# An attention-plus-rational kernel: rational part in four VectorE steps between copies, loads issued first, edge zeroing moved to VectorE, last batch copied by ScalarE

## The chip, the cores and the metric

The kernel runs on one core of one Trainium2 chip. The metric is the device time of one execution in microseconds (us); lower is better. Most executions of a kernel agree within 1%. A traced execution's span is about 1.8 us shorter than the time that is measured for it, because the time also counts what lies outside the span.

## The reference, cut to what matters

Eight batches, twelve heads, 448 positions, head dimension 64. Softmax attention with an extra term in the denominator, then a two-layer block with a rational function in the middle.

```python
scores = scale * q @ k^T                  # per batch and head, 448 x 448
e = exp(scores - m)
attn = e / (sum(e) + exp(-m) + 1e-9)
x = (attn @ v)                            # heads side by side: 3584 x 768
h = x @ w_in                              # 3584 x 2048
P = a[0] + a[1]*h + a[2]*h**2 + a[3]*h**3
Q = 1 + |b[0]|*|h| + |b[1]|*h**2
out = (P / (Q + 1e-6)) @ w_out            # 3584 x 768
```

## The kernel before

A list of work items with times is sorted, and this fixes the program order; TensorE (PE) and ScalarE (ACT) keep that order, while the framework's scheduler orders VectorE (DVE), GpSimd (POOL) and SyncE (SP). So the source alone does not tell where an instruction lands in VectorE's or GpSimd's queue; the compiled program does. Six pairs of heads per batch are one unit of attention; the first GEMM of batch b runs beside the attention of batch b+1, the second GEMM a batch later.

Batches 0 and 1 are transposed on TensorE. From batch 2 on, GpSimd loads k and q (`k4`, `q4`) and SyncE transposes them by DMA into `kT` and `qT`. `q4` has a zero column block at each end. It is zeroed again each time that a batch gets a new `q4` from the pool of two, so the zeroing has to wait until the buffer's former contents have been read:

```python
def load(b, h0=0, h1=H):
    if h0 == 0:
        q4 = ld.tile([T, D + H * NJ * D + D], F16, tag="q4", name="q4")   # pool ld: bufs=2
        nc.gpsimd.memset(q4[:, 0:D], 0.0)
        nc.gpsimd.memset(q4[:, D + H * NJ * D:], 0.0)
        ...                                  # k4, v4, qT, kT: 2 buffers each
    nc.gpsimd.dma_start(out=k4..., in_=runs(k))
    nc.gpsimd.dma_start(out=q4[:, D + h0 * w:D + h1 * w]..., in_=runs(q))
    nc.gpsimd.dma_start(out=v4..., in_=runs(v))

def transpose_dma(b):                        # on SyncE, in order
    nc.sync.dma_start_transpose(out=kT..., in_=k4)
    nc.sync.dma_start_transpose(out=qT[:, T:]..., in_=q4[:, D:D + H * NJ * D])
    nc.sync.dma_start_transpose(out=qT[:, 0:2 * nb * T]..., in_=q4[:, 0:H * NJ * D])
    nc.sync.dma_start_transpose(out=qT[:, 2 * nb * T:]..., in_=q4[:, H * NJ * D:])
```

VectorE copies the first GEMM's result from PSUM, the memory that holds the kernel's matmul results (`h<-hp`), multiplies the attention output by the reciprocal denominator (`xt<-u,rden`), computes the rational part's polynomials on groups of four column blocks (eight instructions, plus `g<-w,c`), and copies the second GEMM's result (`osb<-op`). `hp`, `op` and the transposes share a pool of two PSUM buffers; `u` has one.

```python
    h = hts[b][:, fc % FG, :]
    if b < B - 1 or fc % 2:
        nc.vector.tensor_copy(out=h, in_=hp[:, 0:S])
    else:
        nc.scalar.activation(out=h, in_=hp[:, 0:S], func=AF.Copy)
    ...                                      # every fourth fc: denominator(), eight VectorE instructions
# the schedule
work.append((n - 0.7, transpose_pair, (b, p)))         # b < 2
work.append((n + 1.02, attend, (b, p)))
work.append((t0 + fc * NP / NFC, gemm1, (b, fc)))
work.append((1.0, load_w_out, ()))
```

The softmax here doesn't subtract the row's maximum and nothing guards it: scores larger than these inputs give would overflow.

Of the kernel before, what the change touches and what calls it, by code (L numbers as in the profile page):

```python
# [9 lines left out]
F16 = mybir.dt.float16  # L10
U16 = mybir.dt.uint16
AF = mybir.ActivationFunctionType
ALU = mybir.AluOpType
# [3 lines left out]
def kernel(  # L17
# [11 lines left out]
    nc = tc.nc  # L29

    B, H, S, D = q.shape
    DM, FF = moe_w_in.shape
    NP = H // 2
    NJ = 4
    T = S // NJ
    assert T <= 128 and T % 16 == 0 and D == 64
    NFC = FF // 128
    NDC = DM // 128
    HD = DM // 2
    FG = 4  # L40
# [12 lines left out]
    moe = ctx.enter_context(tc.tile_pool(name="moe", bufs=2))  # L53
# [9 lines left out]
    def load(b, h0=0, h1=H):  # L63
        if h0 == 0:
            q4 = ld.tile([T, D + H * NJ * D + D], F16, tag="q4", name="q4")
            nc.gpsimd.memset(q4[:, 0:D], 0.0)
            nc.gpsimd.memset(q4[:, D + H * NJ * D:], 0.0)
            loaded[b] = (
                q4,
                ld.tile([T, H * NJ * D], F16, tag="k4", name="k4"),  # L70
                ld.tile([T, H, NJ, D], F16, tag="v4", name="v4", bufs=2),
                ld.tile([128, (1 + H * NJ) * T], F16, tag="qT", name="qT", bufs=2),
                ld.tile([128, H * NJ // 2 * T], F16, tag="kT", name="kT", bufs=2),
            )
        q4, k4, v4, _, _ = loaded[b]
        w = NJ * D

        def runs(src):
            return src[b, h0:h1].rearrange("h (p j) d -> p h (j d)", j=NJ)

        nc.gpsimd.dma_start(
            out=k4[:, h0 * w:h1 * w].rearrange("p (h x) -> p h x", x=w), in_=runs(k))
        nc.gpsimd.dma_start(
            out=q4[:, D + h0 * w:D + h1 * w].rearrange("p (h x) -> p h x", x=w),
            in_=runs(q))
        nc.gpsimd.dma_start(
            out=v4[:, h0:h1].rearrange("p h j d -> p h (j d)"), in_=runs(v))
# [21 lines left out]
    def transpose_pair(b, p):  # L109
# [12 lines left out]
                                k4[:, 2 * g * D:(2 * g + 2) * D], ident[0:T, 0:T])  # L122
        nc.vector.tensor_copy(out=kT[:, 4 * p * T:4 * (p + 1) * T], in_=tk)  # L123


    ones = const.tile([T, 64], F16)
    nc.vector.memset(ones, 1.0)
    ident = const.tile([128, 128], F16)
    make_identity(nc, ident)
    abc = const.tile([128, 4], F32)  # L130
    nc.sync.dma_start(out=abc, in_=moe_a.unsqueeze(0).to_broadcast([128, 4]))
    bbc = const.tile([128, 2], F32)
# [3 lines left out]
        out=babs, in0=bbc, scalar1=-1.0, scalar2=None, op0=ALU.mult  # L136
# [6 lines left out]
    a0, a1, a2, a3 = (abc[:, i:i + 1] for i in range(4))  # L143
# [5 lines left out]
    def load_w_in(i, n):  # L149
        f = slice(FF * i // n, FF * (i + 1) // n)  # L150
        nc.gpsimd.dma_start(
            out=w_in_sb[:, :, f],
            in_=moe_w_in[:, f].rearrange("(c p) f -> p c f", p=128))
# [51 lines left out]
    hts = {}  # L205

    def gemm1(b, fc):
        xt = xts[b]
        hp = ps.tile([128, 512], F32, tag="gen", bufs=2, name="hp")
        for c in range(NDC):  # L210
            nc.tensor.matmul(  # L211
                out=hp[:, 0:S], lhsT=w_in_sb[:, c, fc * 128:(fc + 1) * 128],
                rhs=xt[:, c, :], start=(c == 0), stop=(c == NDC - 1),
            )
        if fc % FG == 0:
            hts[b] = moe.tile([128, FG, S], F16, tag="h", name="h")
            gs[b, fc // FG] = gp.tile([128, FG, S], F16, tag="g", name="g")
        h = hts[b][:, fc % FG, :]
        if b < B - 1 or fc % 2:
            nc.vector.tensor_copy(out=h, in_=hp[:, 0:S])  # L220
        else:
            nc.scalar.activation(out=h, in_=hp[:, 0:S], func=AF.Copy)
        for f0, n in groups(b, fc // FG):
            if fc % FG == f0 + n - 1:
                denominator(b, fc // FG, f0, n)


    def groups(b, gi):
        last = b == B - 1 and gi == NG - 1
        return [(0, FG // 2), (FG // 2, FG // 2)] if last else [(0, FG)]  # L230

    cs = {}
    ns = {}


    def denominator(b, gi, f0, n):
        f = slice(f0, f0 + n)
        h = hts[b][:, f, :]
        w = moe.tile([128, FG, S], F16, tag="w", name="w")[:, f, :]
        c = moe.tile([128, FG, S], F16, tag="c", name="c")[:, f, :]  # L240
        nc.vector.tensor_scalar(out=w.bitcast(U16), in0=h.bitcast(U16),
                                scalar1=0x7FFF, scalar2=None, op0=ALU.bitwise_and)
        nc.vector.tensor_scalar(out=c, in0=w, scalar1=b1, scalar2=b0,  # L243
                                op0=ALU.mult, op1=ALU.add)
        nc.vector.tensor_tensor(out=c, in0=c, in1=w, op=ALU.mult)  # L245
        n = w
        nc.vector.tensor_scalar(out=n, in0=h, scalar1=a3, scalar2=a2,  # L247
                                op0=ALU.mult, op1=ALU.add)
        nc.vector.tensor_tensor(out=n, in0=n, in1=h, op=ALU.mult)  # L249
        nc.vector.tensor_scalar(out=n, in0=n, scalar1=a1, scalar2=None, op0=ALU.add)  # L250
        nc.vector.tensor_tensor(out=n, in0=n, in1=h, op=ALU.mult)  # L251
        nc.vector.tensor_scalar(out=n, in0=n, scalar1=a0, scalar2=None, op0=ALU.add)
        cs[b, gi, f0] = c
        ns[b, gi, f0] = n


    def log(b, gi, f0, n):
# [23 lines left out]
    def store(b, c0, n, src):  # L281
        dst = out[b * S:(b + 1) * S, :].rearrange("(p j) d -> j p d", j=NJ)
        r = 0
        while r < n:
            j, p0 = divmod(c0 + r, T)
            m = min(T - p0, n - r)
            nc.sync.dma_start(out=dst[j, p0:p0 + m], in_=src[r:r + m, :])
            r += m

    def gemm2(b, tl, nh):  # L290
        if tl < NW:
            def lhs(fc):
                return gs[b, fc // FG][:, fc % FG, tl * 128:(tl + 1) * 128]
        else:
            def lhs(fc):
                return gxs[b][:, fc, :]
        if nh == 0:
            osbs[b, tl] = moe.tile([128, DM], F32, tag="osb", name="osb")
        osb = osbs[b, tl]
        op = ps.tile([128, 512], F32, tag="gen", bufs=2, name="op")  # L300
        for fc in range(NFC):
            nc.tensor.matmul(  # L302
                out=op[:, 0:HD], lhsT=lhs(fc),
                rhs=w_out_sb[:, fc, nh * HD:(nh + 1) * HD],
                start=(fc == 0), stop=(fc == NFC - 1),
            )
        nc.vector.tensor_copy(out=osb[:, nh * HD:(nh + 1) * HD], in_=op[:, 0:HD])  # L307
        if nh == 1:
            if tl < NW:
                store(b, tl * 128, 128, osb)  # L310
            else:
                store(b - 1, SM, SR, osb[0:SR])
                store(b, SM, SR, osb[SR:128])
# [1 line left out]



    for h0 in range(0, H, 3):
        load(0, h0, h0 + 3)
    load_w_in(0, 2)  # L320
    load(1, 0, 6)
    load_w_in(1, 2)
    load(1, 6, H)


    slots = [n + o for n in range(B * NP) for o in (0.1, 0.6)]
    slots += [B * NP + 0.5 + 0.25 * i for i in range(60)]

    work = []
    for b in range(B):  # L330
        if b >= 2:
            work.append((b * NP - NP - 1.5, load, (b,)))
            work.append((b * NP - NP - 1.49, transpose_dma, (b,)))
        for p in range(NP):
            n = b * NP + p
            if b < 2:
                work.append((n - 0.7, transpose_pair, (b, p)))
            for at, h, i in ((0.0, 2 * p, 0), (0.0, 2 * p, 1),
                             (0.5, 2 * p + 1, 0), (0.5, 2 * p + 1, 1)):
                work.append((n + at, scores, (b, h, i)))  # L340
            work.append((n + 1.02, attend, (b, p)))
        t0 = (b + 1) * NP + 1.4
        for fc in range(NFC):
            work.append((t0 + fc * NP / NFC, gemm1, (b, fc)))
            for f0, n in groups(b, fc // FG):
                if fc % FG == f0 + n - 1:
                    ready = t0 + fc * NP / NFC + 0.3
                    for step in (log, quotient):
                        while slots[0] < ready:
                            slots.pop(0)  # L350
                        work.append((slots.pop(0), step, (b, fc // FG, f0, n)))
        t0 = (b + 2) * NP + 3.0
        work.append((t0 - 0.1, left_over, (b,)))
        tiles = list(range(NW)) + ([NW] if b % 2 else [])
        units = [(b, tl, nh) for tl in tiles for nh in range(2)]
        for i, args in enumerate(units):
            work.append((t0 + i * NP / len(units), gemm2, args))
# [34 lines left out]
```

## Time and profile before

| | before |
|---|---|
| time, median of 4 runs | 504.42 us (502.55 to 506.12) |
| span of the traced run | 501.8 us |
| TensorE busy | 455.0 us, 91% |
| VectorE busy | 374.5 us, 75% |
| ScalarE busy | 326.7 us, 65% |

TensorE bounds the kernel. The page's second part shows the span in 40 equal slices (a digit is the busy share in tenths, 9 is 90% or more). It is full from the eighth slice (about 88 us) on, but for the end. It loses time before that, above all in the first 60 us, where the DMA engines are busy for nine tenths of the time or more, and again near the end, where VectorE is the full one:

```profile
PE   3877978999999999999999999999999999999785
DVE  1223579998969688796969688886969689899921
DMA  9999999998598109931681109811011101111122
```

The waits table (who waited <- for whom: us in total, times, longest us) has these lines for GpSimd. Its zeroing of `q4` (L66) waits for DMA transposes of an earlier batch: `q_420` is batch 2, `q_885` batch 3, `q_1384` batch 4, `q_1979` batch 5, `q_2576` batch 6, `q_3171` batch 7.

```profile
POOL q_1979 L66 <- DMA qT<-q_885: 23.4, 1, 23.4
POOL q_885 L66 <- DMA qT<-q_420: 16.3, 1, 16.3
POOL q_2576 L66 <- DMA qT<-q_1384: 14.3, 1, 14.3
POOL q_3171 L66 <- DMA qT<-q_1979: 13.1, 1, 13.1
```

GpSimd has little else to do (10% busy), so these 67 us cost little there. When the transposes land is shown by the chain of waits in order of time (start us, duration us, what), for batch 2, followed by the first scores that use them. Batch 2's k takes 26.56 us to land; its transposes land at 85.96 us; TensorE's first scores of batch 2 start at 86.09 us, after a wait of 1.2 us:

```profile
33.90 26.56 DMA k_423<-in_k_dram
60.48 4.29 SPq L96
64.82 3.73 SPq L98
68.59 17.37 DMA qT<-q_420
86.09 0.41 PE sps L170 x2
```

For the last batch, the stretches view (from:to and length, then busy us of each engine with the number of instructions, the granted TensorE clock, DMA share and GB/s) shows VectorE full and then TensorE at 0.79 of its clock:

```profile
455.00:470.00 15.00, 11.53 (x66) 6.17 (x64) 14.93 (x24) 7.29 (x8) 1.58 (x2) 1.00 0.09 27
470.00:478.00 8.00, 6.19 (x28) 3.09 (x26) 6.77 (x14) 1.99 (x2) 0.00 (x0) 0.79 0.17 49
```

### The profile page before, as it was taken

The numbers are of one execution on the slowest core, as the hardware profiler recorded it, in microseconds if no ns is written. First come the engines' busy times: TensorE is split into PE (matmuls) and PEld (weight loads), VectorE is DVE, ScalarE is ACT, GpSimd is POOL, SyncE is SP. The second block draws the span as 40 slices with busy tenths as digits, with TensorE's granted clock in tenths as the row PEclk, the third lists the DMA queues.
The fourth block names the chain that finished last, engine by engine and source line by source line (L and its number), as shares of the span: only waits on it lengthen the run. The fifth ranks groups of instructions, "written<-read, shape, count | busy, mean of one in ns | idle before, by whom it ended". The sixth has DMA issues, their size and how long they took to land.

```text
span 501.8 us, 7259 instructions
## 1 busy us (share of the span) xinstructions
PE 455.0 (91%) x2962; PEld 225.6 (45%) x2962; DVE 374.5 (75%) x550; ACT 326.7 (65%) x363; POOL 52.3 (10%) x93
## 2 busy tenths in 40 slices
PE   3877978999999999999999999999999999999785
PEld 2343434445444444444444444444444444555353
DVE  1223579998969688796969688886969689899921
ACT  2797668887776876667776876667776864336300
POOL 9410010401101001010010000010000000100000
PEclk9999989999999999999999999999999999999899
DMA  9999999998598109931681109811011101111122
GB/s 123 206 205 208 204 156 177 161 169 145 110 147 141 31 3 175 186 67 31 98 157 33 33 0 166 122 31 33 2 32 33 31 1 31 45 51 33 30 65 63
DMA packets 91089, 46.85 MB, mean 93 GB/s; under 512 B 51632, under 2 KB 85936, under 8 KB 91056
## 3 DMA queue, kind: packets, MB, share of 16 engines
q0 software_dynamic: 36464, 22.81, 33.3%
q1 hardware_dynamic: 54592, 23.58, 23.9%
q8 instruction: 23, 0.38, 0.3%
q14 instruction: 10, 0.08, 0.0%
HBM read 45.62 MB, written 11.01 MB: 113 GB/s over the span
## 4 chain that ended last, share of the span: by engine, by line
PE 42%; DVE 27%; ACT 13%; DMA 10%; issue 5%; SPq 2%; POOL 1%; DVEq 0%; POOLq 0%
PE op L302 21%; PE hp L211 10%; ACT e L175 6%; DMA k_423<-in_k_dram 5%; DVE h L220 5%; PE sps L170 4%; PE den L188 4%; DMA qT<-q_420 3%; DVE c L245 3%; PE u L188 3%; DVE w L249 3%; DVE xt L199 2%; DVE osb L307 2%; ACT c L263 2%; DVE c L243 2%
## 5 line engine op out<-in xcount | busy, mean ns | idle before, releaser
L175 ACT ACTIVATE e<-sps 112x896 f16<-112x896 f32 x192 | 164.4, 912 | 105.2 <-PE sps L170 105.0
L211 PE MATMUL hp<-xt,w_in_sb 128*128 128x448 f16 x768 | 163.4, 354 | 5.6 <-DVE qT L117 2.7
L302 PE MATMUL op<-w_out_sb,g 128*128 128x384 f16 x768 | 133.4, 329 | 14.5 <-DVE h L220 9.5
L211 PEld LDWEIGHTS <-w_in_sb 128*128 128x128 f16 x768 | 68.4, 97 | 90.6 <-issue 37.3
L302 PEld LDWEIGHTS <-g 128*128 128x128 f16 x768 | 75.5, 98 | 71.4 <-issue 20.0
L220 DVE CAST h<-hp 128x448 f16<-128x448 f32 x120 | 72.9, 618 | 8.9 <-PE hp L211 8.3
L170 PE MATMUL sps<-qT,kT 64*112 64x448 f16 x384 | 61.9, 384 | 12.0 <-DVE kT L123 4.7
L199 DVE TENSOR_TENSOR xt<-u,rden 128x448 f16<-128x448 f32 x48 | 29.8, 621 | 55.7 <-ACT rden L196 23.3
L259 ACT ACTIVATE c<-c,oneeps_c 128x1792 f16<-128x1792 f16 (+1 forms) x33 | 57.3, 1737 | 20.5 <-DVE c L245 20.5
L264 DVE TENSOR_TENSOR g<-w,c 128x1792 f16<-128x1792 f16 (+1 forms) x33 | 35.4, 1074 | 25.5 <-issue 15.4
L263 ACT ACTIVATE c<-c 128x1792 f16<-128x1792 f16 (+1 forms) x33 | 54.2, 1644 | 0.2
L188 PE MATMUL den<-e,ones 112*64 112x448 f16 x384 | 47.0, 368 | 0.0
L307 DVE COPY osb<-op 128x384 f32<-128x384 f32 x56 | 30.9, 552 | 18.0 <-PE op L302 16.6
L170 PEld LDWEIGHTS <-kT 64*112 64x112 f16 x384 | 20.0, 127 | 48.2 <-issue 37.7
L278 POOL COPY gx<-g 128x256 f16<-128x256 f16 x32 | 15.5, 504 | 229.5 <-DVE g L264 203.1
L245 DVE TENSOR_TENSOR c<-c,w 128x1792 f16<-128x1792 f16 (+1 forms) x33 | 35.2, 1067 | 1.0
L251 DVE TENSOR_TENSOR w<-w,h 128x1792 f16<-128x1792 f16 (+1 forms) x33 | 35.1, 1063 | 0.8
L249 DVE TENSOR_TENSOR w<-w,h 128x1792 f16<-128x1792 f16 (+1 forms) x33 | 34.9, 1057 | 0.5
L195 ACT ACTIVATE rden<-den,one_c 128x448 f32<-128x448 f32 x48 | 30.8, 642 | 5.2 <-PE den L188 5.2
L196 ACT ACTIVATE rden<-rden 128x448 f32<-128x448 f32 x48 | 27.7, 577 | 1.5
L188 PEld LDWEIGHTS <-ones 112*64 112x64 f16 x384 | 18.0, 111 | 22.1 <-issue 15.1
L247 DVE TENSOR_SCALAR w<-h,abc 128x1792 f16<-128x1792 f16 (+1 forms) x33 | 24.2, 732 | 0.7
(87 smaller groups left out, 269.2 us busy)
## 6 DMA issues: line engine op xcount, KB each, us to landing
w_in_sb<-in_moe_w_in_dram POOLq DMA_DIRECT2D x2, 1536.0 KB, 18.0
w_out_sb<-in_moe_w_out_dram POOLq DMA_DIRECT2D x1, 3072.0 KB, 32.9
out_dram<-osb SPq DMA_DIRECT2D x8, 336.0 KB, 2.7
out_dram<-osb SPq DMA_DIRECT2D x8, 288.0 KB, 4.1
out_dram<-osb SPq DMA_DIRECT2D x8, 240.0 KB, 2.6
out_dram<-osb SPq DMA_DIRECT2D x8, 192.0 KB, 2.7
out_dram<-osb SPq DMA_DIRECT2D x8, 144.0 KB, 2.5
out_dram<-osb SPq DMA_DIRECT2D x8, 96.0 KB, 3.9
```

The lines of the kernel that those rows point to most:

```text
L170: nc.tensor.matmul(out=sps[0:T, half, 0:S], lhsT=kT[r, (2 * h + i) * T:(2 * h + i + 1) * T], rhs=qT[r, c:c + S], start=True, stop=True,)
L175: nc.scalar.activation(out=e, in_=sps[0:T, :, 0:S], func=AF.Exp, scale=scale)
L188: nc.tensor.matmul(out=dst[64 * hh:64 * hh + 64, 0:S], lhsT=w(hh, j), rhs=e[hh, j // 2][:, j % 2, :], start=(j == 0), stop=(j == NJ - 1), ...
L199: nc.vector.tensor_tensor(out=xts[b][:, p, :], in0=u[:, 0:S], in1=rden, op=ALU.mult)
L211: nc.tensor.matmul(out=hp[:, 0:S], lhsT=w_in_sb[:, c, fc * 128:(fc + 1) * 128], rhs=xt[:, c, :], start=(c == 0), stop=(c == NDC - 1),)
L220: nc.vector.tensor_copy(out=h, in_=hp[:, 0:S])
L245: nc.vector.tensor_tensor(out=c, in0=c, in1=w, op=ALU.mult)
L249: nc.vector.tensor_tensor(out=n, in0=n, in1=h, op=ALU.mult)
L259: nc.scalar.activation(out=c, in_=c, func=AF.Ln, bias=oneeps_c)
L263: nc.scalar.activation(out=c, in_=c, func=AF.Exp, scale=-1.0)
L302: nc.tensor.matmul(out=op[:, 0:HD], lhsT=lhs(fc), rhs=w_out_sb[:, fc, nh * HD:(nh + 1) * HD], start=(fc == 0), stop=(fc == NFC - 1),)
L307: nc.vector.tensor_copy(out=osb[:, nh * HD:(nh + 1) * HD], in_=op[:, 0:HD])
```

## The change

Its intent: PSUM copies should not wait behind eight rational instructions in a row, so the rational part becomes four items placed between copies; loads start before the constants are made; transposes move a little earlier; in the last batch, where VectorE is full, ScalarE takes all copies, and the first GEMM is drawn together so that more of the second GEMM is left to cover the last rational part. The zeroing of `q4` goes to VectorE so that GpSimd is free to issue loads.

```diff
-            nc.gpsimd.memset(q4[:, 0:D], 0.0)
-            nc.gpsimd.memset(q4[:, D + H * NJ * D:], 0.0)
+            nc.vector.memset(q4[:, 0:D], 0.0)
+            nc.vector.memset(q4[:, D + H * NJ * D:], 0.0)
 ...
+    load(0, 0, 3)                       # ahead of the constants; the other three thirds behind ident
 ...
-        if b < B - 1 or fc % 2:
+        if b < B - 1:
             nc.vector.tensor_copy(out=h, in_=hp[:, 0:S])
         else:
             nc.scalar.activation(out=h, in_=hp[:, 0:S], func=AF.Copy)
-        for f0, n in groups(b, fc // FG):
-            if fc % FG == f0 + n - 1:
-                denominator(b, fc // FG, f0, n)
 ...                                     # denominator() cut into den_0, den_1, num_0, num_1
-        nc.vector.tensor_copy(out=osb[:, nh * HD:(nh + 1) * HD], in_=op[:, 0:HD])
+        o = osb[:, nh * HD:(nh + 1) * HD]
+        if b < B - 1:
+            nc.vector.tensor_copy(out=o, in_=op[:, 0:HD])
+        else:
+            nc.scalar.activation(out=o, in_=op[:, 0:HD], func=AF.Copy)
 ...
-                work.append((n - 0.7, transpose_pair, (b, p)))
+                work.append((n - 0.95, transpose_pair, (b, p)))
 ...
+        step1 = NP / NFC if b < B - 1 else 0.3
         for fc in range(NFC):
-            work.append((t0 + fc * NP / NFC, gemm1, (b, fc)))
+            work.append((t0 + fc * step1, gemm1, (b, fc)))
 ...
+                    for dt, part in ((0.02, den_0), (0.1, den_1), (0.4, num_0),
+                                     (0.75, num_1)):
+                        work.append((t + dt * (n / FG), part, args))
```

Before the run, the compiled program could already be read. This is VectorE's queue in the changed kernel, by position; `DMAHW` are semaphores of SyncE's DMAs, `DMASW` of GpSimd's. Position 34 is batch 3's zeroing. It waits for batch 2's q load and its three q transposes, because batch 3's `q4` was given batch 2's buffer, and it stands ahead of batch 1's first `xt`:

```
32 L117 TensorCopy qT<-tq 128x896 [waits PE]
33 L123 TensorCopy kT<-tk 128x448 [waits PE]
34 L66 Memset q_882 112x32 [waits DMAHW4,DMAHW3,DMAHW5,DMASW6,DVE]
35 L67 Memset q_882 112x32
36 L203 TensorTensor xt<-u,rden 128x448 [waits PE,Activation]
37 L117 TensorCopy qT<-tq 128x896 [waits PE]
```

More of the change, by code (lines that the diff above doesn't have):

```diff
@@ L129 @@
     make_identity(nc, ident)
+    for h0 in range(3, H, 3):
+        load(0, h0, h0 + 3)
     abc = const.tile([128, 4], F32)
@@ L215, in gemm1 @@
         if fc % FG == 0:
-            hts[b] = moe.tile([128, FG, S], F16, tag="h", name="h")
+            hts[b, fc // FG] = moe.tile([128, FG, S], F16, tag="h", name="h")
             gs[b, fc // FG] = gp.tile([128, FG, S], F16, tag="g", name="g")
-        h = hts[b][:, fc % FG, :]
-        if b < B - 1 or fc % 2:
+        h = hts[b, fc // FG][:, fc % FG, :]
+        if b < B - 1:
             nc.vector.tensor_copy(out=h, in_=hp[:, 0:S])
@@ L233, with chunk, temp, den_0 @@
     ns = {}
-    def denominator(b, gi, f0, n):
-        f = slice(f0, f0 + n)
-        h = hts[b][:, f, :]
-        w = moe.tile([128, FG, S], F16, tag="w", name="w")[:, f, :]
-        c = moe.tile([128, FG, S], F16, tag="c", name="c")[:, f, :]
+    def chunk(b, gi, f0, n):
+        return hts[b, gi][:, f0:f0 + n, :]
+    def temp(tag, f0, n):
+        return moe.tile([128, FG, S], F16, tag=tag, name=tag)[:, f0:f0 + n, :]
+    def den_0(b, gi, f0, n):
+        h, w, c = chunk(b, gi, f0, n), temp("w", f0, n), temp("c", f0, n)
         nc.vector.tensor_scalar(out=w.bitcast(U16), in0=h.bitcast(U16),
@@ L244, in denominator, with den_1, num_0, num_1 @@
                                 op0=ALU.mult, op1=ALU.add)
-        nc.vector.tensor_tensor(out=c, in0=c, in1=w, op=ALU.mult)
-        n = w
-        nc.vector.tensor_scalar(out=n, in0=h, scalar1=a3, scalar2=a2,
-                                op0=ALU.mult, op1=ALU.add)
-        nc.vector.tensor_tensor(out=n, in0=n, in1=h, op=ALU.mult)
-        nc.vector.tensor_scalar(out=n, in0=n, scalar1=a1, scalar2=None, op0=ALU.add)
-        nc.vector.tensor_tensor(out=n, in0=n, in1=h, op=ALU.mult)
-        nc.vector.tensor_scalar(out=n, in0=n, scalar1=a0, scalar2=None, op0=ALU.add)
-        cs[b, gi, f0] = c
-        ns[b, gi, f0] = n
+        ns[b, gi, f0] = w
+        cs[b, gi, f0] = c
+    def den_1(b, gi, f0, n):
+        c = cs[b, gi, f0]
+        nc.vector.tensor_tensor(out=c, in0=c, in1=ns[b, gi, f0], op=ALU.mult)
+    def num_0(b, gi, f0, n):
+        h, m = chunk(b, gi, f0, n), ns[b, gi, f0]
+        nc.vector.tensor_scalar(out=m, in0=h, scalar1=a3, scalar2=a2,
+                                op0=ALU.mult, op1=ALU.add)
+        nc.vector.tensor_tensor(out=m, in0=m, in1=h, op=ALU.mult)
+    def num_1(b, gi, f0, n):
+        h, m = chunk(b, gi, f0, n), ns[b, gi, f0]
+        nc.vector.tensor_scalar(out=m, in0=m, scalar1=a1, scalar2=None, op0=ALU.add)
+        nc.vector.tensor_tensor(out=m, in0=m, in1=h, op=ALU.mult)
+        nc.vector.tensor_scalar(out=m, in0=m, scalar1=a0, scalar2=None, op0=ALU.add)
     def log(b, gi, f0, n):
@@ L313, in gemm2 @@
                 store(b, SM, SR, osb[SR:128])
-    for h0 in range(0, H, 3):
-        load(0, h0, h0 + 3)
     load_w_in(0, 2)
@@ L342 @@
         t0 = (b + 1) * NP + 1.4
+        step1 = NP / NFC if b < B - 1 else 0.3
         for fc in range(NFC):
-            work.append((t0 + fc * NP / NFC, gemm1, (b, fc)))
+            work.append((t0 + fc * step1, gemm1, (b, fc)))
             for f0, n in groups(b, fc // FG):
                 if fc % FG == f0 + n - 1:
-                    ready = t0 + fc * NP / NFC + 0.3
+                    args = (b, fc // FG, f0, n)
+                    t = t0 + fc * step1
+                    for dt, part in ((0.02, den_0), (0.1, den_1), (0.4, num_0),
+                                     (0.75, num_1)):
+                        work.append((t + dt * (n / FG), part, args))
+                    ready = t + 0.5 * n / FG
                     for step in (log, quotient):
@@ L350 @@
                             slots.pop(0)
-                        work.append((slots.pop(0), step, (b, fc // FG, f0, n)))
+                        work.append((slots.pop(0), step, args))
         t0 = (b + 2) * NP + 3.0
```

## The prediction

> **What bounds the kernel now.** TensorE: 455.0 us busy of a 501.8 us span (page, part 1), about 58 of every 60 us between 100 and 400 us (stretches). VectorE is 75% busy. TensorE loses time in the first 60 us, and at the end, where VectorE bounds (14.93 of 15 us busy at 455 to 470 us; TensorE waits 2.99 and 1.82 us, then runs 28 matmuls in 6.39 us instead of about 4.5).
>
> **What the change is meant to give.** Steady state: little. By the compiled order TensorE's sequence is nearly the same up to the last batch, and VectorE's queue already had the rational steps between copies; the waits open to gain (op on h 9.9 us in the waits table, osb 5.6 us) may shrink by 2 us. End: ScalarE takes 8 more h copies (0.62 us each on VectorE) and the last 8 osb copies (0.55 us), and more second-GEMM work covers the last rational chain: 3 to 8 us less. Start: first load 0.7 us sooner.
>
> **What it costs.** The zeroing of q4's edges moves from GpSimd to VectorE. Under 0.2 us per batch itself, but it must wait until the buffer's old contents have been read. In the before trace GpSimd waits there harmlessly: 16.3, 23.4, 14.3 and 13.1 us, each ended by the DMA transposes of an earlier batch's q (waits table). The compiled order keeps these waits and puts them early into VectorE's queue: batch 3's memset right behind the PSUM copies of batch 1's second pair, ahead of batch 1's first xt multiply; batches 5, 6, 7 two to six instructions behind the last xt of batches 1, 2, 3. The Trainium skill, "TensorE: Matmul & The Clock Gate" (Architectural detail), says VectorE is strictly FIFO; so everything behind stops.
>
> - Batch 3: VectorE arrives at about 45 us; the transposes of batch 2 land at 86.3 us in the before trace, held by DMA loads (batch 2's k lands at 60.5 us), which the change doesn't speed up. TensorE stops at its first first-GEMM unit (49.3 us before, for want of a PSUM buffer) and resumes near 87: 38 us lost.
> - Batch 5: the transposes start when batch 1's last scores free kT (82.5 us in before's time) and take about 24 us; VectorE arrives some 10 us after that start. TensorE loses about 11 us.
> - Batches 6, 7: transposes 129.9 to 153.2 and 186.9 to 208.8 us; VectorE arrives near 141 and 198 us. Stalls of 12 and 11 us; TensorE loses 9 to 10 each.
> - After each stop TensorE runs about 4 us at half speed (same page, "The HAM clock gate": cold after an idle window of about 3.4 us; this trace agrees: den x8 takes 1.71 us early on, 0.95 later): 1.5 to 2 us each.
>
> TensorE has no slack to recover, so all is on the critical path. 38 + 11 + 10 + 9 + 7 = 75 us, less about 9 us at end and start, and 1 to 3 us of DMA waits that vanish: 503 + 63 = 566 us.
>
> **What the profile would show.** Waits table: VectorE memset of q4 waiting on DMA qT, once about 40 us and three times 8 to 14. TensorE idle from about 50 to 86 us; short gaps in the next 130 us; VectorE's busy sum hardly changed; no VectorE-bound stretch at the end.
>
> **What would make it wrong.** Transposes that land much sooner, now that q loads are no longer held; VectorE working off its backlog within TensorE's slack, halving the three later losses; ScalarE's last copies stuck behind its logarithms, eating the gain at the end.
>
> Predicted 566 us, 546 to 584 eight times in ten. Faster by over 2%: 0.04; within 2%: 0.03; slower: 0.93.

## The result, and the profile after

The changed kernel takes 565.62 us (median of 4 runs, 565.39 to 566.46) against 504.42 us, a ratio of 1.1217 (95% interval 1.1167 to 1.1268): 12% slower.

| | before | after |
|---|---|---|
| time | 504.42 us | 565.62 us |
| span of the traced run | 501.8 us | 564.0 us |
| TensorE busy | 455.0 us, 91% | 460.2 us, 82% |
| VectorE busy | 374.5 us, 75% | 366.4 us, 65% |
| mean granted TensorE clock | 0.992 | 0.934 |

VectorE has 8 us less to do and ScalarE 7 us more (333.7 us), the copies of the last batch; TensorE's 5 us more are the same 2962 matmuls, some at a lower clock. None of that is 61 us. The slices show a hole of three slices near the start, and three shallower dents behind it (in both PE and DVE):

```profile
PE   4873009883799769995999999999999999998896
DVE  1231004991989459782788888787878887989920
```

The waits table now has the zeroing's waits on VectorE (`q_882` is batch 3, `q_1976` batch 5, `q_2573` batch 6, `q_3168` batch 7), and TensorE waiting behind it:

```profile
DVE q_882 L66 <- DMA qT<-q_420: 39.4, 1, 39.4
DVE q_1976 L66 <- DMA qT<-q_882: 12.6, 1, 12.6
DVE q_2573 L66 <- DMA qT<-q_1381: 12.4, 1, 12.4
DVE q_3168 L66 <- DMA qT<-q_1976: 10.5, 1, 10.5
PE hp L215 <- DVE qT L117: 39.1, 4, 37.4
PE hp L215 <- DVE h L224: 26.5, 3, 12.1
```

The first stop in the timeline (start us, duration us, engine, line, operation, and in brackets the idle time before it and what ended it). VectorE does its last copy at 44.27 us; the memset, which takes 0.09 us itself, runs at 84.08 us; TensorE resumes at 85.38 us, and its six matmuls take 2.40 us, where they took 1.29 us in the kernel before:

```profile
44.27 0.38 DVE L123 COPY kT<-tk 128x448 f16<-128x448 f16 x1
47.66 0.36 PE L121 MATMUL tk<-ident,k_120 112*128 112x112 f16 x4
84.08 0.09 DVE L66 MEMSET q_882<- 112x32 uint32 x1 [39.43 <-DMA qT<-q_420]
84.17 0.62 DVE L203 TENSOR_TENSOR xt<-u,rden 128x448 f16<-128x448 f32 x1
85.38 2.40 PE L215 MATMUL hp<-xt,w_in_sb 128*128 128x448 f16 x6 [37.36 <-DVE qT L117]
```

How much each stop cost can be read from one recurring event: SyncE starts the transposes of batch b+2 when batch b's last scores have freed `kT`. The starts, from SyncE's timeline:

| kT transpose of batch | before | after | later by | added since the line above |
|---|---|---|---|---|
| 3 (batch 1's scores done) | 82.51 | 117.75 | 35.24 | 35.2: first stop |
| 4 (batch 2's) | 129.86 | 178.07 | 48.21 | 13.0: second |
| 5 (batch 3's) | 186.89 | 245.24 | 58.35 | 10.1: third |
| 6 (batch 4's) | 243.04 | 309.53 | 66.49 | 8.1: fourth |
| 7 (batch 5's) | 300.01 | 366.51 | 66.50 | 0.0 |

The four stops cost 66.5 us; the spans differ by 62.2 us, so 4.3 us were won back, all in the last batch (the last `u` group is still 66.5 us late, at 485.48 against 418.98 us). In the steady stretch the change gains nothing at all. This is one such stretch of the kernel before and its counterpart after, 42.23 us each, with the same busy time to the hundredth on every engine:

```profile
257.78:300.01 42.23, 41.06 (x269) 19.89 (x266) 33.69 (x49) 30.42 (x35) 0.81 (x2) 1.00 0.15 36
```

```profile
324.28:366.51 42.23, 41.06 (x269) 19.89 (x266) 33.69 (x49) 30.42 (x35) 0.81 (x2) 1.00 0.17 37
```

### The profile page after: what moved, and what is told of

Same layout as the page of the kernel before. It is cut to its first block, busy times and chain, and to the rows that moved or that the text cites. A ratio compares the mean times of both kernels' runs of the same rounds, so it can differ in the third digit from the quotient of the medians.

```text
span 564.0 us, 7256 instructions
## 1 busy us (share of the span) xinstructions
PE 460.2 (82%) x2962; PEld 227.0 (40%) x2962; DVE 366.4 (65%) x550; ACT 333.7 (59%) x379; POOL 50.5 (9%) x77
## 4 chain that ended last, share of the span: by engine, by line
PE 38%; DVE 23%; DMA 12%; SPq 10%; ACT 9%; issue 5%; POOL 2%; DVEq 0%; POOLq 0%
PE op L314 17%; PE hp L215 13%; SPq L101 6%; DMA k_423<-in_k_dram 5%; ACT e L179 4%; DVE h L224 4%; PE sps L174 3%; PE den L192 3%; DVE c L253 3%; DMA k_120<-in_k_dram 3%; SPq L98 2%; DVE w L260 2%; PE u L192 2%; ACT c L275 2%; DVE g L276 2%
## 5 line engine op out<-in xcount | busy, mean ns | idle before, releaser
L215 PE MATMUL hp<-xt,w_in_sb 128*128 128x448 f16 x768 | 170.0, 365 | 68.2 <-DVE qT L117 39.1
L314 PE MATMUL op<-w_out_sb,g 128*128 128x384 f16 x768 | 131.5, 326 | 12.2 <-DVE h L224 9.9
L215 PEld LDWEIGHTS <-w_in_sb 128*128 128x128 f16 x768 | 70.5, 100 | 157.0 <-issue 106.4
L224 DVE CAST h<-hp 128x448 f16<-128x448 f32 x112 | 68.3, 618 | 10.6 <-PE hp L215 10.0
L174 PE MATMUL sps<-qT,kT 64*112 64x448 f16 x384 | 62.2, 386 | 11.0 <-ACT e L179 4.8
L192 PEld LDWEIGHTS <-ones 112*64 112x64 f16 x384 | 17.9, 110 | 22.3 <-issue 15.3
L321 DVE COPY osb<-op 128x384 f32<-128x384 f32 x48 | 26.4, 550 | 0.7 <-PE op L314 0.7
L66 DVE MEMSET q_882<- 112x32 uint32 x1 | 0.1, 85 | 39.4 <-DMA qT<-q_420 39.4
```

The source lines that it names most:

```text
L174: nc.tensor.matmul(out=sps[0:T, half, 0:S], lhsT=kT[r, (2 * h + i) * T:(2 * h + i + 1) * T], rhs=qT[r, c:c + S], start=True, stop=True,)
L192: nc.tensor.matmul(out=dst[64 * hh:64 * hh + 64, 0:S], lhsT=w(hh, j), rhs=e[hh, j // 2][:, j % 2, :], start=(j == 0), stop=(j == NJ - 1), ...
L215: nc.tensor.matmul(out=hp[:, 0:S], lhsT=w_in_sb[:, c, fc * 128:(fc + 1) * 128], rhs=xt[:, c, :], start=(c == 0), stop=(c == NDC - 1),)
L314: nc.tensor.matmul(out=op[:, 0:HD], lhsT=lhs(fc), rhs=w_out_sb[:, fc, nh * HD:(nh + 1) * HD], start=(fc == 0), stop=(fc == NFC - 1),)
```

## The experiments

Theory: the time is lost because the zeroing's wait for DMA transposes now stands in VectorE's queue, which is strictly in order; what it costs is set by when those transposes land. Rivals: the new order of rational steps and copies, or ScalarE's copies, cost the time; or there is a fixed cost of zeroing on VectorE. Ten kernels were run; all gave correct results.

### e1: the zeroing back on GpSimd, all else as changed

```diff
-            nc.vector.memset(q4[:, 0:D], 0.0)
-            nc.vector.memset(q4[:, D + H * NJ * D:], 0.0)
+            nc.gpsimd.memset(q4[:, 0:D], 0.0)
+            nc.gpsimd.memset(q4[:, D + H * NJ * D:], 0.0)
```

> The changed kernel with one thing undone: the zeroing of q4's edges is back on GpSimd. Theory (the waits of the memset stop VectorE's queue): the 66.5 us lost between 45 and 310 us vanish, the 4 us won at the end stay: 496 to 500 us; no VectorE wait on a DMA transpose; GpSimd waits 10 to 25 us on them again. Rival (the new order of the rational steps, or ScalarE's copies, cost the time, and VectorE's waits only show up where TensorE would have waited anyway): above 550 us.

Measured: 501.65 us (500.66 to 502.18, 6 runs), ratio 0.996 (0.9942 to 0.9978). The loss is gone with this one edit, and the rival falls. But the time misses the upper end of the expectation by 1.7 us. The waits table tells where a part of it went: TensorE now waits 4.9 us for batch 2's transposes, where the kernel before waited 1.2 us. Above it stands GpSimd's line; it waits again, as expected:

```profile
POOL q L66 <- DMA qT<-q: 67.2, 4, 24.1
PE sps L174 <- DMA qT<-q: 4.9, 1, 4.9
```

### e2: the kernel before with the zeroing on VectorE

The reverse edit, on the kernel before.

> The kernel before with one thing done: the zeroing moved to VectorE, nothing else. Theory: 503 plus about 66 us, 566 to 573 us, with VectorE waits on DMA transposes of about 40, 12, 12 and 10 us. Rival: within 1% of 503 us.

Measured: 571.31 us (570.05 to 572.9, 4 runs), ratio 1.1335 (1.1304 to 1.1366). As the theory has it; the four waits are 38.4, 11.5, 12.4 and 11.3 us. The two lines that move the zeroing make the whole loss, without any other part of the change.

### e3: two q4 buffers kept for the whole run and zeroed once, on VectorE

```diff
+    q4s = []
+    for i in range(2):
+        q4s.append(const.tile([T, D + H * NJ * D + D], F16, name=f"q4{i}"))
+        nc.vector.memset(q4s[i][:, 0:D], 0.0)
+        nc.vector.memset(q4s[i][:, D + H * NJ * D:], 0.0)
 ...
-            q4 = ld.tile([T, D + H * NJ * D + D], F16, tag="q4", name="q4")
-            nc.vector.memset(q4[:, 0:D], 0.0)
-            nc.vector.memset(q4[:, D + H * NJ * D:], 0.0)
+            q4 = q4s[b % 2]
```

> The changed kernel with two q4 buffers that are kept for the whole run and zeroed once at the start, on VectorE, so that the zeroing never has to wait for a reader. Theory (the wait costs, not the engine): as fast as the kernel with the zeroing on GpSimd, within 2 us, 495 to 500 us, and no VectorE wait on a DMA transpose; batch 3's q load starts tens of us sooner and batch 2's first scores still wait about 1 us, which is all that could be won. Rival (VectorE's small memsets themselves disturb): clearly slower than that one.

Measured: 499.43 us (496.05 to 501.77, 6 runs), ratio 0.991 (0.9876 to 0.9944). VectorE still does the zeroing, but without a wait, and nothing is lost: it is the wait and not the engine. It is 2.2 us faster than e1, where a difference within 2 us was expected; so nothing here suggests that e1's four waits on GpSimd cost more than that. Another part of the expectation missed. Batch 3's q load did not start sooner: it was issued at 87.48 us, because the scheduler put batch 4's q load ahead of it into GpSimd's queue, and that one waits for batch 2's transposes (until 86.21 us). TensorE's wait for batch 2's transposes is 4.2 us, not about 1 us.

### e4: as e1, and the last batch as before

```diff
-        if b < B - 1:
+        if b < B - 1 or fc % 2:                      # gemm1: VectorE shares the copies
-        if b < B - 1:                                # gemm2: all osb copies on VectorE
-        step1 = NP / NFC if b < B - 1 else 0.3
+        step1 = NP / NFC
```

> The changed kernel with the zeroing on GpSimd and the last batch as before (VectorE shares its copies, the first GEMM not drawn together). Theory: the whole gain of the other parts sits in the last batch: 4 us slower than with the zeroing on GpSimd alone, so 502 to 503.5 us, the same as before. Rival: the four-part rational brings the gain in the steady stretch; then it stays near 498 us.

Measured: 504.71 us (503.71 to 506.84, 6 runs), ratio 1.0025 (1.0002 to 1.0048). It is 3.1 us slower than e1 and a shade slower than the kernel before, 1.2 us above the range that was expected. The last batch holds all of the gain; the rest of the change (early loads, earlier transposes, four rational pieces) gains nothing, and by the interval may cost 0.25%.

### e5: changed kernel, w_out's load behind batch 2's k, q and v

The aim was to leave VectorE's queue as it is and let batch 2's transposes land sooner.

```diff
-    work.append((1.0, load_w_out, ()))
+    work.append((NP - 1.48, load_w_out, ()))
-    with tc.manual_schedule(engines={PE, Activation}):
+    with tc.manual_schedule(engines={PE, Activation, Pool}):
```

> The changed kernel, zeroing still on VectorE and its queue's order the same, but GpSimd issues the loads in the program's order and w_out's load comes behind batch 2's k, q and v instead of ahead of them, so that batch 2's transposes should land some 20 to 25 us sooner (about 60 to 64 us instead of 84). Theory (the first stop lasts until those transposes land): the wait of batch 3's memset falls from 39.4 to 15 to 20 us, the other three stay at 10 to 13 us, and the time falls by about 22 us, to 540 to 547 us. Rival (a fixed cost of the zeroing on VectorE): no change, 565 us.

Measured: 552.12 us (550.89 to 553.64, 4 runs), ratio 1.0961 (1.093 to 1.0993): neither expectation. Batch 2's k did land sooner, at 45.5 instead of 60.2 us, but the transposes then ran beside w_out's load (issued at 43.28 us), and SyncE spent 14.43 and 14.71 us on the first two instead of 4.23 and 3.37 us. They landed no sooner, and the first wait was 41.5 us. SyncE's timeline:

```profile
45.54 14.43 SPq L96 DMA_TRANSPOSE kT<-k  x1
60.01 14.71 SPq L98 DMA_TRANSPOSE qT<-q  x1
74.76 7.09 SPq L101 DMA_TRANSPOSE qT<-q  x1
81.90 1.23 SPq L105 DMA_TRANSPOSE qT<-q  x1
```

The 13.5 us that it gained came from the other three stops (counted by the starts of the kT transposes they became 4.9, 3.9 and 5.9 us cheaper, and the first 0.6 us dearer): VectorE's waits fell to 7.2, 8.3 and 6.6 us, and TensorE's waits behind them from 12.1, 8.1 and 6.3 us to 6.7, 4.0 and 2.4 us, together 13.4 us. With GpSimd in program order the loads of later batches are issued later (batch 4's q at 152.62 us, 109.78 in the changed kernel), so fewer of them run beside those transposes: batch 3's took 17.9 us from the start of kT to the landing, 23.2 us in the changed kernel. That fits the theory, that the wait's end is the landing, but the run did not test what it was built to test.

### e6: the zeroing on VectorE only up to batch 3

```diff
+            edge = nc.vector if b <= 3 else nc.gpsimd
+            edge.memset(...)                          # both memsets
```

> The changed kernel with the zeroing on VectorE for batches 0 to 3 only, GpSimd for batches 4 to 7. Theory (the four stops add up): only the first stop is left, 39 us long, so 565.6 less the 31 us that the later three cost, 531 to 537 us. Rival (one stop sets everything off and the later ones are its echo, or TensorE's slack absorbs them): below 515 or above 550 us.

Measured: 534.35 us (533.71 to 534.46, 4 runs), ratio 1.0603 (1.0572 to 1.0635), in the range. One wait is left on VectorE, of 40.1 us. The changed kernel's other three stops are worth 565.62 - 534.35 = 31.3 us, and the table above gave 13.0 + 10.1 + 8.1 = 31.2 us. The stops add up; TensorE has no slack that would absorb them.

### e7: as e3, with e5's order of loads

> The kernel that zeroes two kept q4 buffers once, with GpSimd issuing the loads in the program's order and w_out's load behind batch 2's k, q and v. Theory (in the kernels without the stop, TensorE's gain in the first 80 us is given back at a 4 to 5 us wait of batch 2's first scores for its transposes, and 2 us at half clock behind it): the wait vanishes, 491 to 496 us, against 499.4 without the reorder. Rival (the start is bound by something else): within 1 us of 499.4 us.

Measured: 499.24 us (497.48 to 504.74, 6 runs), ratio 0.9923 (0.9883 to 0.9964). The wait did not vanish; it fell to 2.6 us, since the transposes were slowed by w_out's load just as in e5. The time is that of e3. The expectation missed for the reason that e5 showed.

### e8: as e5, but w_out's load waits until batch 2's transposes have landed

```diff
+        if b == 3:                                   # in load(), behind q's DMA and ahead of v's
+            load_w_out()
-    work.append((1.0, load_w_out, ()))
```

> The changed kernel, zeroing on VectorE in the same place of its queue; w_out's load now waits until batch 2's transposes have landed (issued behind batch 3's q load), so that it can't slow them as it did in e5. Theory (the first stop ends when batch 2's transposes land): k lands at 45 us as in e5, the transposes take 15 to 20 us, the first wait is 17 to 24 us instead of 39 to 41, the later ones 6 to 9 us as in e5, and the time falls by 17 to 24 us against e5, to 528 to 536 us. Rival (a fixed cost): the first wait stays near 40 us and the time at 552 us.

Measured: 533.38 us (532.06 to 534.54, 4 runs), ratio 1.0579 (1.0556 to 1.0602). Against e5 this is 18.7 us less, and the first wait fell from 41.5 to 24.15 us, 17.4 us less (its expected range ended at 24); the later three are 6.9, 8.1 and 6.7 us, as expected. The compiled order of VectorE's queue is that of the changed kernel but for one `xt` that changed places with its neighbour. Now the transposes take 7.84, 3.41 and 7.36 us, and the zeroing runs at 68.25 us:

```profile
46.58 7.84 SPq L98 DMA_TRANSPOSE kT<-k  x1
54.47 3.41 SPq L100 DMA_TRANSPOSE qT<-q  x1
57.92 7.36 SPq L103 DMA_TRANSPOSE qT<-q  x1
65.32 1.23 SPq L107 DMA_TRANSPOSE qT<-q  x1
```

```profile
68.25 0.09 DVE L66 MEMSET q<- 112x32 uint32 x1 [24.15 <-DMA qT<-q]
```

This is the test that e5 was to be. The first stop is as long as batch 2's transposes are late; and next to each other, e5 and e8 show that with the 3 MB load beside them the first two transposes took 6.6 and 11.3 us longer.

### e9: as e3, with e8's order of loads

> The best version in sight: two kept q4 buffers zeroed once, loads in program order, w_out's load behind batch 3's q. Theory: batch 2's transposes land near 62 us, long before its first scores (80 us), so that TensorE's 4 us wait and the half clock behind it go: 491 to 496 us. Risk: w_out lands near 90 to 95 us, and slows batch 3's transposes; it is first needed at about 106 us. Rival: within 1 us of 499.4 us.

Measured: 497.11 us (496.54 to 499.55, 6 runs), ratio 0.9858 (0.984 to 0.9875). It is the fastest kernel, 1.4% faster than the one before, though 1.1 us above the expected range. TensorE's wait for DMA transposes is gone from the waits table. The risk came true without harm: w_out's load (74.89 to 98.7 us) ran beside batch 3's kT transpose, which took 14.46 us (6.80 us in e3), but TensorE's waits table shows no wait for it. Five of the six runs lie between 496.54 and 497.24 us; the traced one, 499.55 us, is the slowest, so this trace can't be used to tell where the last microsecond went.

### e10: the kernel before with only the last batch changed

h and osb copies of batch 7 by ScalarE, first GEMM of batch 7 at a step of 0.3; the rational part in one piece.

> The kernel before with only the last batch changed as the change has it: h and osb copies by ScalarE, the first GEMM drawn together; rational part in one piece, zeroing on GpSimd. Theory (all that the change gains sits in the last batch): 3 to 4 us faster, 499.5 to 501 us. Rival (the four pieces of the rational part are needed for it): within 1 us of 503.5 us.

Measured: 500.06 us (498.67 to 503.17, 6 runs), ratio 0.9929 (0.9903 to 0.9955). As expected: three small edits in the last batch bring what the change has to give, and the four pieces are not needed for it.

| kernel | time | ratio to before |
|---|---|---|
| changed kernel | 565.62 | 1.1217 |
| e1 zeroing on GpSimd | 501.65 | 0.996 |
| e2 before, zeroing on VectorE | 571.31 | 1.1335 |
| e3 zeroed once | 499.43 | 0.991 |
| e4 as e1, last batch as before | 504.71 | 1.0025 |
| e5 w_out later | 552.12 | 1.0961 |
| e6 VectorE up to batch 3 | 534.35 | 1.0603 |
| e7 zeroed once, w_out later | 499.24 | 0.9923 |
| e8 w_out behind the transposes | 533.38 | 1.0579 |
| e9 zeroed once, w_out behind | 497.11 | 0.9858 |
| e10 before, last batch changed | 500.06 | 0.9929 |

## Why the prediction was right

The time was predicted at 566 us and measured at 565.62 us. The mechanism was right. That the number fits to 0.4 us is luck: the stops were put 8.5 us too high, what is taken off them 6 to 8 us too high, and the start was 503 us where 504.42 us was measured (the medians differ by 61.2 us, not 63).

| term | predicted | measured |
|---|---|---|
| first stop: VectorE's wait | about 40 us | 39.4 us |
| later waits | 8 to 14 us, three times | 12.6, 12.4, 10.5 us |
| TensorE idle in the four stops | 38, 11, 10, 9 us | 37.4, 12.1, 8.1, 6.3 us |
| half clock behind them | 7 us in all | 8.6 us in all, from the slower groups below |
| stops together | 75 us | 66.5 us |
| end, start and DMA waits that vanish | 10 to 12 us | 4.3 us, at the end |
| sum | +63 us | +62.2 us (spans) |

- *Bound and steady state.* "Steady state: little" was right; the measured gain is zero, shown by the two equal stretches.
- *The wait in VectorE's queue.* This rested on the compiled order, on GpSimd's waits in the trace before, and on the Trainium skill, "TensorE: Matmul & The Clock Gate" (Architectural detail), which calls VectorE strictly FIFO. The trace agrees: between the copy at 44.27 us and the memset at 84.08 us VectorE executes nothing, though the operands of `xt` were ready. e1, e2 and e3 show that this is the whole loss; e8 shows that the landing sets its length.
- *When the transposes land.* The step "which the change doesn't speed up" held: 84.0 us against 86.0 us.
- *Half clock.* The skill's clock gate ("TensorE: Matmul & The Clock Gate", The HAM clock gate: half rate after an idle window) was right in direction. After the first stop, two groups of six first-GEMM matmuls took 2.40 and 2.31 us, after the second stop one took 2.40 us, where 1.29 to 1.31 us is usual; after the third and fourth, twelve took 4.56 and 4.59 us instead of 2.44 us. With the scores and denominator groups next to them (0.99 instead of 0.58 us, 1.30 instead of 0.95 us) the excess is about 2.5, 1.9, 2.1 and 2.1 us.
- *Stops oversized.* 75 us was the sum of gross terms. The gross terms measured, 63.9 us of idle time and 8.6 us of half clock, make 72.5 us; the net loss is 66.5 us. The kernel before also lost time in the stretch of the first stop, and the prediction did not subtract that: from 47.7 to 82.5 us its TensorE waits add up to 5.1 us, and behind one of them, 1.68 us long, its matmuls ran at half clock and lost 1.6 us more (lines below). The changed kernel has 2.0 us of such waits left there: 37.4 + 2.5 + 2.0 - 5.1 - 1.6 = 35.2 us, as the table of starts has it. At the other three stops together the gross terms exceed the net loss by 1.4 us, which are not assigned. The later two stops cost 10.1 and 8.1 us instead of about 12 and 11 us: at the third, VectorE stopped at 189.33 us, but TensorE went on to 194.3 us, with a second-GEMM unit, four scores and a whole group of denominator and attention matmuls that needed nothing more of VectorE. The kernel before, in the stretch of the first stop:

```profile
65.53 0.36 PE L121 MATMUL tk<-ident,k_120 112*128 112x112 f16 x4 [1.68 <-DVE h L220]
66.66 1.65 PE L211 MATMUL hp<-xt,w_in_sb 128*128 128x448 f16 x6 [0.25 <-DVE qT L117]
68.24 0.99 PE L170 MATMUL sps<-qT,kT 64*112 64x448 f16 x4
69.17 1.71 PE L188 MATMUL den<-e,ones 112*64 112x448 f16 x8
70.66 1.04 PE L188 MATMUL u<-e,v_121 112*64 112x448 f16 x8
```

- *The gain at the end.* "3 to 8 us less" at the end measured 4.3 us. "No VectorE-bound stretch at the end" was wrong. VectorE is busy 19.63 of 20 us from 520 us on, with the rational part and four copies of batch 6's second GEMM (0.55 us each):

```profile
520.00:540.00 20.00, 17.48 (x101) 9.84 (x101) 19.63 (x34) 9.80 (x12) 1.48 (x2) 1.00 0.09 25
```

- *Start.* "First load 0.7 us sooner" was wrong: it was issued at 1.28 instead of 1.55 us, and TensorE's wait for the first q was 6.9 us instead of 6.6 us. Nothing was gained there.
- *DMA waits that vanish.* Right in the changed kernel, where TensorE arrives too late to wait. But without the stop the same wait grows: 4.9 us in e1 instead of 1.2 us. This was not foreseen in the expectation of e1.

Left open: why e4, which has all but the last batch of the change and no stop, is 1.4 us slower than the kernel before rather than equal. The traces show where. By the starts of the kT transposes, e4 is 3.2 us ahead at batch 3 (79.30 against 82.51 us) and 0.7 us behind at batch 4 (130.58 against 129.86 us). In between lie batch 2's first scores: they wait 2.75 us for their transposes instead of 1.24 us, and in e4 the four groups from there on run at half clock and lose 3.0 us. So, as far as one trace each shows, e4 comes 3.2 us earlier to transposes that land only 1.7 us earlier, and loses more at the wait than it had gained. e9, where this wait is gone, is 2.3 us faster than e3, which fits; no run takes it out of e4. How a further cut of that start would pay, beyond e9, was not tried either.

## What to carry to other kernels

Moving an instruction to another engine moves its wait too. On an engine with nothing else to do, a wait of 16 us cost little; in the queue of an in-order engine that feeds TensorE, a memset of 0.09 us with a wait in front of it cost 35 us. So before moving a "cheap" instruction, look at what it waits for and at the position the scheduler gives it, and prefer to take the wait away (zero once, keep the buffer) over moving it. And when a load is moved out of the way of another transfer, check what it runs beside afterwards.

## What the Trainium skill lacked or had wrong

- "DMA: Bandwidth & Descriptors" (Rules for kernel authors) says that a DMA transpose next to ordinary DMAs "needs nothing". That line is about results, and these were correct in all runs; no figure for the time is beside it. Beside w_out's load SyncE spent 14.43 and 14.71 us on two transposes (e5), against 7.84 and 3.41 us with that load moved behind them (e8).
- "TensorE: Matmul & The Clock Gate" (The HAM clock gate) gives an idle window of about 3.4 us as what turns the clock down. Here shorter waits did: behind a wait of 2.99 us in the kernel before, 28 matmuls took 6.39 us instead of about 4.7 us (an estimate: 37 of them took 6.19 us at 478.01 us), behind one of 2.62 us in e7 four scores matmuls took 0.99 us instead of 0.58 us, and soon after one of 1.68 us in the kernel before the same four took 0.99 us too (lines above). Behind one of 2.36 us in e5 the clock was full (1.30 us for six first-GEMM matmuls). So in these runs the length of the last wait alone does not decide it.
- No page on VectorE says that its queue is strictly in order, which decided this (39.4 us in the longest wait); the remark stands in the page on TensorE, in a sentence on queue depths.
